# An adaptive-layernorm attention block on one core: five K accumulators for six, silu's steps on GpSimd, Q's weights as whole rows, the gate batch by batch

## The chip, the core and the metric

The kernel runs on one core of a Trainium2 chip. A core has five engines that run side by side, each with its own queue of instructions: TensorE (PE: matmuls, with weight loads shown as PEld), VectorE (DVE), ScalarE (ACT), GpSimd (POOL) and SyncE (SP), which here only issues DMAs. Matmuls write to PSUM, which this kernel uses as eight banks of 128 partitions x 512 fp32; all else lies in SBUF. The metric is the device time of one execution in microseconds.

## The reference

`x` is 2 x 256 x 1152 (B, N, D), `c` is 2 x 1152, all in bf16. The weights are `wqkv` (1152 x 3456), `wo` (1152 x 1152) and `w_mod` (1152 x 6912).

```python
mod = (silu(c) @ w_mod).reshape(B, 6, 1, D)
shift_a, scale_a, gate_a, shift_m, scale_m, gate_m = [mod[:, i] for i in range(6)]
h = layernorm(x, axis=-1) * (1 + scale_a) + shift_a
qkv = h @ wqkv
q, k, v = qkv[..., :D], qkv[..., D:2*D], qkv[..., 2*D:]
p = softmax(einsum('bqd,bkd->bqk', q, k) * D ** (-0.5), axis=-1)
a = einsum('bqk,bkd->bqd', p, v) @ wo
return x + gate_a * a
```

Three of the six rows of `mod` are used: shift, scale and gate of the attention.

## The kernel before

The 512 tokens (two batches of 256) are four tiles of 128; the 1152 features are nine blocks of 128, counted by k on the input side and by f on the output side.

*Front.* Each tile of x is centred (`centre`, line 227, on VectorE, with the mean from `bn` on VectorE or from `act_mean` on ScalarE), turned on TensorE in two halves (`transposes`, 233) and copied to `xcT` (`xcT_copy`, 240). silu(c) is computed by `silu_c` (191): one exponential on ScalarE, then three short VectorE steps, then a ScalarE copy that repeats it into `scT_rep`, the small operand of the modulation matmuls. The scale rows are matmuls of `wS` with it, in three parts of the features, PA (k 0 and 1), PB (2 to 4) and PC (5 to 8): `scale_open`, `scale_rows`, `scale_out`. `scaled` (273) multiplies `xcT` by a block's scale into `hTs`. The factor 1/std is not in it; it is applied later.

*K.* K's output is computed from `hTs` with k outermost, into six PSUM accumulators (`accs`, f 0 to 5). The other three blocks of f are computed for k 0 and 1 at once and parked in SBUF in the tile `held` (`pair_part` for f 6 and 7, `k_block` for f 8), and finished by `held_block` (425) for k 2 to 8. `k_part` runs a slice of tokens for k 0 and 1, `k_step` (292) all 512 tokens of one k.

*h.* 1/std of the four tiles is cut into three bf16 parts on VectorE, turned (`pT3`), masked and spread over the partitions by a matmul (`bc_ps`), and copied to `rstd_bc`, the last row of `held`. Then nine `normalised` steps write `hT`; the shift rows come from 36 matmuls with `wH` into `psH`, a VectorE transpose gives `shT`, and 18 `shifted` steps (VectorE and ScalarE) add them.

*Q, scores, V, output.* Q is nine blocks of nine matmuls (`q_block`, 456), each block to its end before the next. Q's weights and V's lie in six column chunks of 384 (`chunks_w`), loaded by `load_chunk`. Then the scores of both batches, the softmax (`scores`, `exps`, `probs`), whose first product also reads `rstd_bc`, and a DMA transpose (`turn`). Meanwhile TensorE runs twelve V groups, the attention products (`attnT`) and the output projection with `wO`.

*The gate.* `gate_steps` (480) accumulates silu(c) times `wG` on VectorE, nine steps for each batch of 128 x 1152; a GpSimd all-reduce over the partitions then sums it into `gate_bc`. The last 192 columns of the output use `wo_last`, `wO` times the gate, computed on GpSimd.

The order of every engine's instructions is that of the program: each engine's calls are recorded (line 76, which is why all instructions have that line) and pinned by `pin`. PSUM is one pool of six banks and two of one bank each. SyncE issues all large loads in one queue, in this order: x, wS and wK mixed, wH, Q's first chunk, then wG's three parts alternating with Q's other chunks, V's chunks, wO. The tiles `wG` and `wO` take the buffers of `wS` and `wH`, and `gate_bc` that of `held`.

What ties the all-reduces to the gate, on line 555 and following:

```python
    gate_done = dve_seq[-1].ins.name
    gate_bc = act.tile([P, B, D], F32, tag="gb")
    for b in range(B):
        ar = gps.partition_all_reduce(gate_bc[:, b, :], gacc[:, b, :], P, bass.bass_isa.ReduceOp.add)
        tc.add_manual_dep(ar.ins, gate_done, SYNC_SCHED, reason="keep gpsimd off the shared port")
```

Of the kernel before, what the change touches and what calls it, by code (L numbers as in the profile page):

```python
# [16 lines left out]
def kernel(  # L17
# [18 lines left out]
    FB = CW // P  # L36
# [3 lines left out]
    NACC = 6  # L40
    NPAIR = 2
    LASTF = KT - 1
# [58 lines left out]
    def one(t):  # L101
# [32 lines left out]
    chunk_cols = [vc * CW for vc in range(NCH)] + [2 * D + vc * CW for vc in range(NCH)]  # L134
    chunks_w = [wpool.tile([P, KT, CW], BF16, tag=f"wchunk{i}", name="wqv") for i in range(2 * NCH)]
# [15 lines left out]
    def load_chunk(i, k0, k1):  # L151
        c0 = chunk_cols[i]
        spq.dma_start(out=chunks_w[i][:, k0:k1, :], in_=wqkv_v[:, k0:k1, c0 : c0 + CW])
# [20 lines left out]
    load_chunk(0, 0, 5)  # L174
    load_chunk(0, 5, KT)

    junk_ps = psum_b.tile([P, 512], F32, tag="pb", name="junk_ps")
# [6 lines left out]
    e_sb = small.tile([P, B, KT], F32, tag="e_sb")  # L184
    scT_f = const.tile([P, KT, B], F32)
# [47 lines left out]
    def transposes(t, h, pool, tag):  # L233
        k0, k1 = HALF[h]
        tp = pool.tile([P, 5, P], BF16, tag=tag, name="tp")
# [16 lines left out]
    held = act.tile([P, NPAIR + 2, T], F32, tag="gb")  # L252
    rstd_bc = held[:, NPAIR + 1, :]

    psS = {}

    def scale_open(part, pool, tag):
        n = part[1] - part[0]
        ps = pool.tile([P, n, NR], F32, tag=tag, name="psS")
# [4 lines left out]
    def scale_rows(part, kk0, kk1):  # L264
        for kk in range(kk0, kk1):
            for j in range(*part):
                ten.matmul(psS[part][:, j - part[0], :], lhsT=wS[:, kk, j * P : (j + 1) * P], rhs=sc_rhs(kk),
                           start=False, stop=(kk == KT - 1), skip_group_check=True)
# [18 lines left out]
    def pair_part(ps, k, sl):  # L287
        for i in range(NPAIR):
            ten.matmul(ps[:, i, :], lhsT=wk(k, NACC + i), rhs=hTs[:, k, sl],
                       start=(k == 0 and i == 0), stop=(k == KA - 1), skip_group_check=True)  # L290

    def k_step(k):
        for f in range(NACC):
            ten.matmul(accs[f], lhsT=wk(k, f), rhs=hTs[:, k, :],
                       start=False, stop=(k == KT - 1), skip_group_check=True)
# [11 lines left out]
    fillers(11)  # L307
    silu_c()
    mv0 = bn(0)
# [4 lines left out]
    scale_open(PA, psum_a, "pa")  # L314
    transposes(0, 0, psum, "mm")
    transposes(0, 1, psum, "mm")
    fillers(2)
    scale_rows(PA, 0, 4)
    transposes(1, 0, psum, "mm")
    transposes(1, 1, psum, "mm")  # L320
    xcT_copy(0, 0, True)
    xcT_copy(1, 0, True)
    centre(2, nmean[:, 2:3], ALU.add)
    xcT_copy(0, 1, False)
    fillers(2)
    scale_rows(PA, 4, KT)
    xcT_copy(1, 1, False)
    scaled(0, tok(0), psS[PA][:, 0, 0:1])
    scale_out(PA)
    scaled_b(1, 0)  # L330


    accs = [psum.tile([P, T], F32, tag="mm", name="acc") for _ in range(NACC)]
    k_part(0, tok(0))
    transposes(2, 0, psum_b, "pb")
    xcT_copy(2, 0, False)
# [3 lines left out]
    for k in range(KA):  # L340
        scaled(k, one(2), s1p[:, k, 1:2])
# [3 lines left out]
    centre(3, mv3[:, 0:1], ALU.subtract)  # L345
    ps_b0 = psum_a.tile([P, NPAIR, N], F32, tag="pa", name="psE")
    pair_part(ps_b0, 0, tok(0))
    k_part(1, tok(0))
    pair_part(ps_b0, 1, tok(0))
    transposes(2, 1, psum_b, "pb")  # L350
    sca.copy(out=held[:, 0:NPAIR, tok(0)], in_=ps_b0)
    xcT_copy(2, 1, False)
    act_var(1)
    for k in range(KA):
        k_part(k, one(2))


    scale_open(PB, psum_a, "pa")
    scale_rows(PB, 0, 4)
    transposes(3, 0, psum_b, "pb")  # L360
    xcT_copy(3, 0, True)
    scale_rows(PB, 4, KT)
    for k in range(KA):
        scaled(k, one(3), s1p[:, k, 1:2])
    scale_out(PB)
    transposes(3, 1, psum_b, "pb")
    xcT_copy(3, 1, False)
    act_var(2)
    gps.tensor_copy(out=var[:, 0:1], in_=mv0[:, 1:2])
    gps.tensor_copy(out=var[:, 3:4], in_=mv3[:, 1:2])  # L370
    gps.tensor_scalar_add(out=rstd, in0=var, scalar1=EPS)
    gps.tensor_tensor(out=rstd, in0=rstd, in1=neg_half, op=ALU.pow)
    for k in range(KA):
        k_part(k, one(3))
    for k in range(*PB):
        for b in range(B):
            scaled_b(k, b)
    ps_b1 = psum_b.tile([P, NPAIR, N], F32, tag="pb", name="psE")
    for k in range(KA):
        pair_part(ps_b1, k, tok(1))  # L380
    f8 = psum_a.tile([P, T], F32, tag="pa", name="psL")
    k_block(LASTF, f8, 0, KA)
    sca.copy(out=held[:, 0:NPAIR, tok(1)], in_=ps_b1)
    sca.copy(out=held[:, NPAIR, :], in_=f8)


# [3 lines left out]

    parts = const.tile([P, TT, 3], BF16)
    rest = const.tile([P, TT], F32)
    vec.tensor_copy(out=parts[:, :, 0], in_=rstd)
    vec.tensor_tensor(out=rest, in0=rstd, in1=parts[:, :, 0], op=ALU.subtract)
    vec.tensor_copy(out=parts[:, :, 1], in_=rest)
    vec.tensor_tensor(out=rest, in0=rest, in1=parts[:, :, 1], op=ALU.subtract)
    vec.tensor_copy(out=parts[:, :, 2], in_=rest)
    scale_open(PC, psum_b, "pb")
    scale_rows(PC, 0, KT)
    pT3 = psum_a.tile([NP3, P], BF16, tag="pa", name="pT3")  # L400
    ten.transpose(pT3, parts.rearrange("p t i -> p (t i)"), ident)
    masked = const.tile([NP3, TT, P], BF16)
    scale_out(PC)
    for b in range(B):
        scaled_b(PC[0], b)
    vec.tensor_tensor(out=masked, in0=pT3.unsqueeze(1).to_broadcast([NP3, TT, P]), in1=mask, op=ALU.mult)
    for k in range(PC[0] + 1, PC[1]):
        for b in range(B):
            scaled_b(k, b)
    k_step(PC[0] - 1)  # L410
    k_step(PC[0])
    bc_ps = psum_a.tile([P, T], F32, tag="pa", name="bc_ps")
# [8 lines left out]
    for k in range(PC[0] + 1, KT):  # L421
        k_step(k)
    for f in range(NACC):
        evac(False, qkT[:, KT + f, :], accs[f])
    def held_block(i, f, pool, tag):
        ps = pool.tile([P, T], F32, tag=tag, name="psK")
        k_block(f, ps, KA, KT)
        vec.tensor_tensor(out=qkT[:, KT + f, :], in0=ps, in1=held[:, i, :], op=ALU.add)

    held_block(0, NACC, psum_a, "pa")  # L430


    psH = psum_b.tile([P, KT, 32], F32, tag="pb", name="psH")
# [19 lines left out]
    held_block(1, NACC + 1, psum, "mm")  # L453
    held_block(2, LASTF, psum, "mm")

    def q_block(f):
        wt, off = chunks_w[f // FB], f % FB * P
        ps = psum.tile([P, T], F32, tag="mm", name="psQ")
        for k in range(KT):
            ten.matmul(ps, lhsT=wt[:, k, off : off + P], rhs=hT[:, k, :], start=(k == 0), stop=(k == KT - 1))  # L460
        return ps
# [16 lines left out]
    gates = [(b, kt) for g in range(0, KT, 3) for b in range(B) for kt in range(g, g + 3)]  # L478
# [11 lines left out]
    for f in range(KT):  # L490
        evac(False, qkT[:, f, :], q_block(f))
# [3 lines left out]
    for b in range(B):  # L495
        s_ps = psum.tile([P, NQ, N], F32, tag="mm")
# [39 lines left out]
    def v_group(gidx):  # L536
        t, vc = divmod(gidx, NCH)
        wt = chunks_w[NCH + vc]
        ps = psum.tile([P, CW], F32, tag="mm")
# [4 lines left out]
    gate_steps(13)  # L544
# [12 lines left out]
    for b in range(B):  # L557
        ar = gps.partition_all_reduce(gate_bc[:, b, :], gacc[:, b, :], P, bass.bass_isa.ReduceOp.add)
# [93 lines left out]
```

## Time and profile before

| what | value |
|---|---|
| time, median of 3 runs | 98.85 us (98.83 to 100.47) |
| the profiled execution: its own time | 98.85 us |
| its span from first to last instruction | 97.1 us |
| granted TensorE clock in it | 1.0 |
| first K matmul | 9.99 us |
| K's step k=2 begins | 16.45 us |
| shift rows (`psH`) begin | 28.96 us |
| Q begins, ends | 33.21, 50.9 us |
| V groups begin; attention; output projection | 54.6; 72.2; 76.1 us |
| last matmul ends | 93.9 us |

Times in the profile count from the start of the span. A row of a timeline has the start, the time in us, the engine, the line, the operation, output and inputs, the shapes, how many were merged, and in brackets how long the engine was idle before and what ended that. TensorE's matmuls overlap: a row's time is that of the first start to the last end, so starts are what to compare. "SPq" rows are DMA issues; the time to landing is counted from the start of the issue.

### The profile page before, as it was taken

The page shows a single profiled execution, that of the slowest core. Times are in us where ns is not written, and L with a number is a line of the kernel's source. Part 1 is how long each engine was busy: PE and PEld are TensorE (multiplying, and loading weights), DVE is VectorE, ACT ScalarE, POOL GpSimd, SP SyncE. Part 2 cuts the span into 40 slices and gives each one's busy share as a digit, 9 for nine tenths or more (in the row PEclk, how much of TensorE's full clock was granted, in tenths as well). Part 3 has the DMA queues.
Part 4 walks back from the last instruction along what each step waited for, and adds up shares of the span by engine and source line. Part 5 has one row for each costly group of instructions (what it writes and reads, how often), then busy time and mean ns, then how long its engine had stood idle before and what let it go on. Part 6 is the DMA issues. An engine that isn't in the chain of part 4 may idle for free.

```text
span 97.1 us, 1688 instructions
## 1 busy us (share of the span) xinstructions
PE 90.9 (94%) x666; PEld 53.6 (55%) x670; DVE 70.2 (72%) x136; ACT 32.5 (33%) x66; POOL 24.3 (25%) x28
## 2 busy tenths in 40 slices
PE   3979899999999999999999999999999999999960
PEld 1327886463445444444458766656668766666660
DVE  1296876273999999999995899960229587779880
ACT  5098298302094722242221472331115400000000
POOL 6500001600000000000000000029999940059700
PEclk9999999999999999999999999999999999999999
DMA  2999999999999999999999962200000000311212
GB/s 29 336 306 368 352 368 354 387 392 393 392 345 364 350 359 354 356 357 326 330 343 387 390 224 58 54 7 0 0 0 0 0 0 0 128 49 72 108 56 79
DMA packets 18311, 21.31 MB, mean 219 GB/s; under 512 B 2176, under 2 KB 12800, under 8 KB 18304
## 3 DMA queue, kind: packets, MB, share of 16 engines
q1 hardware_dynamic: 17888, 21.19, 65.0%
q8 instruction: 5, 0.08, 0.3%
q10 hardware_dynamic: 416, 0.02, 0.3%
q14 instruction: 2, 0.02, 0.1%
HBM read 19.76 MB, written 1.18 MB: 216 GB/s over the span
## 4 chain that ended last, share of the span: by engine, by line
PE 86%; DVE 5%; DMA 3%; ACT 1%; issue 1%; DVEq 0%
PE ps L76 39%; PE psQ L76 18%; PE acc L76 12%; PE psK L76 5%; PE s_ps L76 4%; DMA c_sb<-in_c_dram 3%; PE tp L76 2%; PE psS L76 2%; DVE stats L76 1%; PE psH L76 1%; PE psE L76 1%; DVE o_sb L76 1%; PE junk_ps L76 1%; DVE ga L76 1%; ACT xcT L76 1%
## 5 line engine op out<-in xcount | busy, mean ns | idle before, releaser
L76 POOL PARTITION_ALL_REDUCE gate_bc<-gacc x2 | 13.7, 6887 | 46.2 <-DVE gacc L76 46.2
L76 DVE SCALAR_TENSOR_TENSOR gacc<-wG,scT_f,gacc 128x1152 f32<-128x1152 bf16 x16 | 22.3, 1417 | 0.4
L76 PE MATMUL ps<-wqv,hT 128*128 128x384 bf16 x108 | 17.7, 326 | 0.0
L76 PE MATMUL psQ<-hT,wqv 128*128 128x512 bf16 x80 | 17.6, 379 | 0.1
L76 PE MATMUL ps<-wO,attnT 128*128 128x384 bf16 (+1 forms) x108 | 17.0, 320 | 0.0
L76 PEld LDWEIGHTS <-attnT 128*128 128x128 bf16 x126 | 11.3, 98 | 6.4
L76 PEld LDWEIGHTS <-hT 128*128 128x128 bf16 x108 | 10.6, 98 | 6.9
L76 PEld LDWEIGHTS <-wK 128*128 128x128 bf16 x109 | 9.4, 98 | 8.1 <-issue 1.1
L76 PE MATMUL acc<-hTs,wK 128*128 128x512 bf16 (+2 forms) x77 | 12.6, 313 | 0.6 <-DVE hTs L76 0.4
L76 PEld LDWEIGHTS <-wqv 128*128 128x128 bf16 x81 | 7.9, 98 | 9.6
L76 ACT CAST qkT<-psQ 128x512 bf16<-128x512 f32 x9 | 5.3, 585 | 12.9 <-PE psQ L76 12.9
L76 DVE TENSOR_TENSOR ga<-ps,gate_bc 128x384 f32<-128x384 f32 (+1 forms) x12 | 6.5, 540 | 3.5 <-PE ps L76 3.5
L76 ACT CAST v_sb<-ps 128x384 bf16<-128x384 f32 x10 | 4.7, 475 | 10.7 <-PE ps L76 10.7
L76 DVE TENSOR_TENSOR o_sb<-ga,x_sb 128x384 bf16<-128x384 f32 (+1 forms) x12 | 7.2, 601 | 0.4
L76 PE MATMUL junk_ps<-junk 128*128 128x512 bf16 x15 | 6.1, 562 | 1.5 <-DVE junk L76 1.5
L76 POOL TENSOR_TENSOR wo_last<-wO,gate_bc 128x192 bf16<-128x192 bf16 x9 | 5.6, 659 | 7.3 <-issue 7.3
L76 DVE TENSOR_TENSOR hT<-hTs,held 128x512 bf16<-128x512 bf16 x9 | 5.5, 688 | 1.6 <-ACT held L76 1.6
L76 ACT CAST o_sb<-ps 128x64 bf16<-128x64 f32 x1 | 0.2, 212 | 17.3 <-PE ps L76 17.3
L76 PEld LDWEIGHTS <-junk 128*128 128x128 bf16 (+2 forms) x19 | 2.1, 121 | 5.8 <-issue 4.2
L76 DVE CAST v_sb<-ps 128x384 bf16<-128x384 f32 x2 | 1.1, 558 | 5.6 <-PE ps L76 5.6
L76 PE MATMUL psK<-hTs,wK 128*128 128x512 bf16 x20 | 4.8, 380 | 0.1
L76 DVE CAST attnT<-ps 128x512 bf16<-128x512 f32 (+1 forms) x6 | 3.5, 603 | 1.7 <-PE ps L76 1.7
(77 smaller groups left out, 87.5 us busy)
## 6 DMA issues: line engine op xcount, KB each, us to landing
wqv<-in_wqkv_dram SPq DMA_DIRECT2D x5, 864.0 KB, 11.3
wH<-in_w_mod_dram SPq DMA_DIRECT2D x3, 864.0 KB, 13.3
wG<-in_w_mod_dram SPq DMA_DIRECT2D x3, 864.0 KB, 12.1
wO<-in_wo_dram SPq DMA_DIRECT2D x3, 864.0 KB, 9.7
wK<-in_wqkv_dram SPq DMA_DIRECT2D x5, 288.0 KB, 6.9
x_sb<-in_x_dram SPq DMA_DIRECT2D x4, 288.0 KB, 3.8
wK<-in_wqkv_dram SPq DMA_DIRECT2D x2, 576.0 KB, 10.4
out_dram<-o_sb SPq DMA_DIRECT2D x3, 288.0 KB, 2.1
```

The lines of the kernel that those rows point to most:

```text
L76: r = fn(*a, **k)
```

## The change

- *PSUM:* five banks in the pool, and three single ones (BA, BB, BC); `bank` hands them out. After the held blocks, Q, scores, V, attention and projection take the eight in a ring.
- *K:* five accumulators; four blocks of f are parked after k 0 and 1, in pairs for each batch, and finished by four held blocks, two before the shift rows and two after.
- *Front:* one filler more at the start and four fewer later. silu's addition, product and copy go from VectorE and ScalarE to GpSimd; the mask is made after them. Tile 2 is turned behind the scale rows of PA. Tile 3's mean comes from a ScalarE sum of 640 columns and a VectorE sum of 512. Tile 2's variance goes from ScalarE to VectorE. PB's and PC's scale rows run in one piece, and 1/std is cut into its parts on GpSimd.
- *Q:* its weights are one tile loaded in three groups of whole rows ahead of wG, and the first four blocks run with k outermost.
- *Gate:* all nine steps of batch 0 come first, and its all-reduce is issued ahead of batch 1's last eight steps; the extra dependency is gone.

```diff
-    NACC = 6
-    NPAIR = 2
-    LASTF = KT - 1
+    NACC = 5
+    NPARK = KT - NACC
...
-    psum = ctx.enter_context(tc.tile_pool(name="psum", bufs=6, space=PSUM))
+    psum = ctx.enter_context(tc.tile_pool(name="psum", bufs=5, space=PSUM))
...
+    psum_c = ctx.enter_context(tc.tile_pool(name="psum_c", bufs=1, space=PSUM))
+    MM, BA, BB, BC = (psum, "mm"), (psum_a, "pa"), (psum_b, "pb"), (psum_c, "pc")
+    ring = [MM] * 5 + [BA, BB, BC]
+    turn_no = [0]
+
+    def bank(shape, name, dtype=None, where=None):
+        if where is None:
+            where = ring[turn_no[0] % len(ring)]
+            turn_no[0] += 1
+        return where[0].tile(shape, dtype or F32, tag=where[1], name=name)
...
+    def load_q(k0, k1):
+        spq.dma_start(out=wQ[:, k0:k1, :], in_=wqkv_v[:, k0:k1, 0:D])
+
+    def load_v(i):
+        c0 = 2 * D + i * CW
+        spq.dma_start(out=chunks_w[i], in_=wqkv_v[:, :, c0 : c0 + CW])
...
-    load_chunk(0, 0, 5)
-    load_chunk(0, 5, KT)
+    for k0, k1 in ((0, 2), (2, 5), (5, KT)):
+        load_q(k0, k1)
...
         sca.activation(out=e_sb, in_=c_sb, func=ACT.Exp, scale=-1.0)
-        vec.tensor_scalar_add(out=e_sb, in0=e_sb, scalar1=1.0)
-        vec.reciprocal(out=e_sb, in_=e_sb)
-        vec.tensor_tensor(out=scT_f.rearrange("p k b -> p b k"), in0=c_sb, in1=e_sb, op=ALU.mult)
-        sca.copy(out=scT_rep, in_=scT_f.unsqueeze(2).to_broadcast([P, KT, NR // B, B]))
+        gps.tensor_scalar_add(out=e_sb, in0=e_sb, scalar1=1.0)
+        vec.reciprocal(out=r_sb, in_=e_sb)
+        gps.tensor_tensor(out=scT_f.rearrange("p k b -> p b k"), in0=c_sb, in1=r_sb, op=ALU.mult)
+        gps.tensor_copy(out=scT_rep, in_=scT_f.unsqueeze(2).to_broadcast([P, KT, NR // B, B]))
...
+    scale_open(PC, BB)
+    scale_rows(PC, 0, KT)
+    scale_out(PC)
+    for k in range(*PC):
         for b in range(B):
             scaled_b(k, b)
...
+    k_step(PC[0] - 1)
+    k_step(PC[0])
+    k_step(PC[0] + 1, 0, 3)
+    pT3 = bank([NP3, P], "pT3", BF16, BA)
...
+    held_block(0, BA)
+    held_block(1, BC)
...
-    load_mod(wG, 2, 0, 3, 0, D)
-    load_chunk(1, 0, KT)
-    load_mod(wG, 2, 3, 6, 0, D)
-    load_chunk(2, 0, KT)
-    load_mod(wG, 2, 6, KT, 0, D)
-    load_chunk(3, 0, KT)
-    load_chunk(4, 0, KT)
-    load_chunk(5, 0, KT)
+    for k0 in range(0, KT, 3):
+        load_mod(wG, 2, k0, k0 + 3, 0, D)
+    for i in range(NCH):
+        load_v(i)
...
-    gates = [(b, kt) for g in range(0, KT, 3) for b in range(B) for kt in range(g, g + 3)]
+    gates = [(b, kt) for b in range(B) for kt in range(KT)]
...
+    QACC = 4
+    q_acc = [bank([P, T], "psQ", where=MM) for _ in range(QACC)]
+    for k in range(KT):
+        for f in range(QACC):
+            ten.matmul(q_acc[f], lhsT=wq(k, f), rhs=hT[:, k, :], start=(k == 0), stop=(k == KT - 1))
...
-    gate_steps(13)
+    gate_bc = act.tile([P, B, D], F32, tag="gb")
+
+    def spread(b):
+        gps.partition_all_reduce(gate_bc[:, b, :], gacc[:, b, :], P, bass.bass_isa.ReduceOp.add)
+
+    gate_steps(9)
     scores(0)
     exps(0)
     scores(1)
...
     gate_steps(1)
     probs(1)
     turn(1)
+    spread(0)
     gate_steps(len(gates))
-    gate_done = dve_seq[-1].ins.name
-    gate_bc = act.tile([P, B, D], F32, tag="gb")
-    for b in range(B):
-        ar = gps.partition_all_reduce(gate_bc[:, b, :], gacc[:, b, :], P, bass.bass_isa.ReduceOp.add)
-        tc.add_manual_dep(ar.ins, gate_done, SYNC_SCHED, reason="keep gpsimd off the shared port")
+    spread(1)
```

More of the change, by code (lines that the diff above doesn't have):

```diff
@@ L231, with transposes @@
     tps = {}
-    def transposes(t, h, pool, tag):
+    def transposes(t, h, where):
         k0, k1 = HALF[h]
-        tp = pool.tile([P, 5, P], BF16, tag=tag, name="tp")
+        tp = bank([P, 5, P], "tp", BF16, where)
         for k in range(k0, k1):
@@ L251, with scale_open @@
     qkT = act.tile([P, 2 * KT, T], BF16)
-    held = act.tile([P, NPAIR + 2, T], F32, tag="gb")
-    rstd_bc = held[:, NPAIR + 1, :]
+    held = act.tile([P, NPARK + 1, T], F32, tag="gb")
+    rstd_bc = held[:, NPARK, :]
     psS = {}
-    def scale_open(part, pool, tag):
+    def scale_open(part, where):
         n = part[1] - part[0]
-        ps = pool.tile([P, n, NR], F32, tag=tag, name="psS")
+        ps = bank([P, n, NR], "psS", where=where)
         ten.matmul(ps.rearrange("p j r -> p (j r)"), lhsT=junk[0:1, :P], rhs=ones_row[0:1, 0 : n * NR],
@@ L262, in scale_open, with scale_rows @@
         psS[part] = ps
[L264 to L268, printed above, removed]
+    def scale_rows(part, kk0, kk1, js=None):
+        for j0, j1 in [part] if js is None else js:
+            for kk in range(kk0, kk1):
+                for j in range(j0, j1):
+                    ten.matmul(psS[part][:, j - part[0], :], lhsT=wS[:, kk, j * P : (j + 1) * P], rhs=sc_rhs(kk),
+                               start=False, stop=(kk == KT - 1), skip_group_check=True)
     def scale_out(part):
@@ L285, in k_part, with pair, pair_part, park @@
                        start=(k == 0 and sl.start == 0), stop=False, skip_group_check=True)
-    def pair_part(ps, k, sl):
-        for i in range(NPAIR):
-            ten.matmul(ps[:, i, :], lhsT=wk(k, NACC + i), rhs=hTs[:, k, sl],
-                       start=(k == 0 and i == 0), stop=(k == KA - 1), skip_group_check=True)
-    def k_step(k):
-        for f in range(NACC):
+    def pair(i, b, where):
+        return bank([P, 2, N], "psE", where=where), NACC + 2 * i, tok(b)
+    def pair_part(pr, k):
+        ps, f0, sl = pr
+        for i in range(2):
+            ten.matmul(ps[:, i, :], lhsT=wk(k, f0 + i), rhs=hTs[:, k, sl],
+                       start=(k == 0 and i == 0), stop=(k == KA - 1), skip_group_check=True)
+    def park(pr):
+        ps, f0, sl = pr
+        sca.copy(out=held[:, f0 - NACC : f0 - NACC + 2, sl], in_=ps)
+    def k_step(k, f0=0, f1=NACC):
+        for f in range(f0, f1):
             ten.matmul(accs[f], lhsT=wk(k, f), rhs=hTs[:, k, :],
@@ L313 @@
     act_mean(2)
[L314 to L317, printed above, removed]
+    scale_open(PA, BA)
+    transposes(0, 0, MM)
+    transposes(0, 1, MM)
+    xcT_copy(0, 0, True)
+    xcT_copy(0, 1, False)
+    transposes(1, 0, MM)
+    transposes(1, 1, MM)
     scale_rows(PA, 0, 4)
-    transposes(1, 0, psum, "mm")
-    transposes(1, 1, psum, "mm")
-    xcT_copy(0, 0, True)
+    centre(2, nmean[:, 2:3], ALU.add)
     xcT_copy(1, 0, True)
[L323 to L326, printed above, removed]
     xcT_copy(1, 1, False)
+    scale_rows(PA, 4, KT, js=[(0, 1), (1, 2)])
     scaled(0, tok(0), psS[PA][:, 0, 0:1])
+    transposes(2, 0, BB)
+    transposes(2, 1, BC)
     scale_out(PA)
-    scaled_b(1, 0)
-    accs = [psum.tile([P, T], F32, tag="mm", name="acc") for _ in range(NACC)]
-    k_part(0, tok(0))
-    transposes(2, 0, psum_b, "pb")
-    xcT_copy(2, 0, False)
+    xcT_copy(2, 0, True)
+    xcT_copy(2, 1, False)
+    scaled(0, one(2), s1p[:, 0, 1:2])
+    scaled(1, tok(0), s1p[:, 1, 0:1])
+    scaled(1, one(2), s1p[:, 1, 1:2])
+    accs = [bank([P, T], "acc", where=MM) for _ in range(NACC)]
+    k_part(0, tok(0))
+    k_part(0, one(2))
+    pr10 = pair(0, 0, BC)
+    pair_part(pr10, 0)
+    H3 = 5 * P
+    sca.activation(out=xc[:, 3, 0:H3], in_=x_sb[:, 3, 0:H3], func=ACT.Copy, accum_out=ssum[3])
+    half3 = small.tile([P, 1], F32, tag="half3", name="half3")
+    vec.reduce_sum(out=half3, in_=x_sb[:, 3, H3:D], axis=AX.X)
+    vec.tensor_scalar(out=nmean[:, 3:4], in0=half3, scalar1=ssum[3], scalar2=-1.0 / D, op0=ALU.add, op1=ALU.mult)
+    centre(3, nmean[:, 3:4], ALU.add)
+    k_part(1, tok(0))
+    pair_part(pr10, 1)
+    k_part(1, one(2))
+    pr20 = pair(1, 0, BA)
+    park(pr10)
+    transposes(3, 0, BB)
+    pair_part(pr20, 0)
+    pair_part(pr20, 1)
+    transposes(3, 1, BC)
+    xcT_copy(3, 0, True)
+    park(pr20)
+    xcT_copy(3, 1, False)
+    for k in range(KA):
+        scaled(k, one(3), s1p[:, k, 1:2])
     st3 = small.tile([P, NCH, 6], F32, tag="stats", name="stats")
@@ L340 @@
     for k in range(KA):
-        scaled(k, one(2), s1p[:, k, 1:2])
+        k_part(k, one(3))
+    scale_open(PB, BA)
+    scale_rows(PB, 0, KT)
+    scale_out(PB)
+    for k in range(*PB):
+        for b in range(B):
+            scaled_b(k, b)
     bn_part(3, st3, 2)
@@ L344 @@
     vec.bn_aggr(out=mv3, in_=st3)
[L345 to L352, printed above, removed]
-    act_var(1)
[L354 to L368, printed above, removed]
+    mv2 = bn(2)
+    pr11, pr21 = pair(0, 1, BB), pair(1, 1, BC)
+    for pr in (pr11, pr21):
+        for k in range(KA):
+            pair_part(pr, k)
+        park(pr)
+    act_var(1)
     gps.tensor_copy(out=var[:, 0:1], in_=mv0[:, 1:2])
     gps.tensor_copy(out=var[:, 3:4], in_=mv3[:, 1:2])
+    gps.tensor_copy(out=var[:, 2:3], in_=mv2[:, 1:2])
@@ L381 @@
[L381 to L384, printed above, removed]
-    for k in range(PB[0], PB[1] - 1):
-        k_step(k)
     parts = const.tile([P, TT, 3], BF16)
     rest = const.tile([P, TT], F32)
-    vec.tensor_copy(out=parts[:, :, 0], in_=rstd)
-    vec.tensor_tensor(out=rest, in0=rstd, in1=parts[:, :, 0], op=ALU.subtract)
-    vec.tensor_copy(out=parts[:, :, 1], in_=rest)
@@ L396 @@
[L396 to L400, printed above, removed]
+    gps.tensor_copy(out=parts[:, :, 0], in_=rstd)
+    gps.tensor_tensor(out=rest, in0=rstd, in1=parts[:, :, 0], op=ALU.subtract)
+    gps.tensor_copy(out=parts[:, :, 1], in_=rest)
+    gps.tensor_tensor(out=rest, in0=rest, in1=parts[:, :, 1], op=ALU.subtract)
@@ L410 @@
-    k_step(PC[0] - 1)
-    k_step(PC[0])
-    bc_ps = psum_a.tile([P, T], F32, tag="pa", name="bc_ps")
+    k_step(PC[0] + 1, 3)
+    k_step(PC[0] + 2, 0, 2)
+    bc_ps = bank([P, T], "bc_ps", where=BC)
     ten.matmul(bc_ps, lhsT=junk[:NP3, :P], rhs=masked.rearrange("p t n -> p (t n)"), start=True, stop=True)
@@ L420 @@
         normalised(k)
-    for k in range(PC[0] + 1, KT):
+    k_step(PC[0] + 2, 2)
+    for k in range(PC[0] + 3, KT):
         k_step(k)
@@ L424, with held_block @@
         evac(False, qkT[:, KT + f, :], accs[f])
[L425 to L433, printed above, removed]
+    def held_block(i, where):
+        ps = bank([P, T], "psK", where=where)
+        k_block(NACC + i, ps, KA, KT)
+        vec.tensor_tensor(out=qkT[:, KT + NACC + i, :], in0=ps, in1=held[:, i, :], op=ALU.add)
+    held_block(0, BA)
+    held_block(1, BC)
+    psH = bank([P, KT, 32], "psH", where=BB)
     wH_v = wH.rearrange("p kk (k j c) -> p kk k j c", k=KT, j=4)
@@ L452, with wq @@
         shifted(i)
[L453 to L461, printed above, removed]
+    held_block(2, MM)
+    held_block(3, BB)
+    def wq(k, f):
+        return wQ[:, k, f * P : (f + 1) * P]
     wG = wmpool.tile([P, KT, D], BF16, tag="wS")
     wO = wmpool.tile([P, KT, D], BF16, tag="wH")
-    load_mod(wG, 2, 0, 3, 0, D)
-    load_chunk(1, 0, KT)
-    load_mod(wG, 2, 3, 6, 0, D)
-    load_chunk(2, 0, KT)
-    load_mod(wG, 2, 6, KT, 0, D)
-    load_chunk(3, 0, KT)
-    load_chunk(4, 0, KT)
-    load_chunk(5, 0, KT)
+    for k0 in range(0, KT, 3):
+        load_mod(wG, 2, k0, k0 + 3, 0, D)
+    for i in range(NCH):
+        load_v(i)
     for k0 in range(0, KT, 3):
@@ L488, in gate_steps @@
                                          in1=gacc[:, b, :], op0=ALU.mult, op1=ALU.add)
-    for f in range(KT):
-        evac(False, qkT[:, f, :], q_block(f))
+    turn_no[0] = 4
+    QACC = 4
[3 more added lines that the diff above has]
+            ten.matmul(q_acc[f], lhsT=wq(k, f), rhs=hT[:, k, :], start=(k == 0), stop=(k == KT - 1))
+    for f in range(QACC):
+        evac(False, qkT[:, f, :], q_acc[f])
+    for f in range(QACC, KT):
+        ps = bank([P, T], "psQ")
+        for k in range(KT):
+            ten.matmul(ps, lhsT=wq(k, f), rhs=hT[:, k, :], start=(k == 0), stop=(k == KT - 1))
+        evac(False, qkT[:, f, :], ps)
     s_tiles = []
     for b in range(B):
-        s_ps = psum.tile([P, NQ, N], F32, tag="mm")
+        s_ps = bank([P, NQ, N], "s_ps")
         for i in range(NQ):
```

56 lines of the change are left out of this document (23 added, 33 removed).

## The prediction, made before the changed kernel ran

> **What bounds the kernel now.** I read the page first (busy shares, the 40 slices), then the chain that ended last, then the DMA issues with their landings, then the timelines of the engines where the diff works.
>
> ```profile
> span 97.1 us, 1688 instructions
> PE 90.9 (94%) x666; PEld 53.6 (55%) x670; DVE 70.2 (72%) x136; ACT 32.5 (33%) x66; POOL 24.3 (25%) x28
> ...
> PE   3979899999999999999999999999999999999960
> ...
> DMA  2999999999999999999999962200000000311212
> ...
> PE 86%; DVE 5%; DMA 3%; ACT 1%; issue 1%; DVEq 0%
> ```
>
> PE is nearly full from slice 4 on and is 86% of the chain; DMA is full to slice 23 (56 us). So up to some point PE may be fed by DMA at its limit. The timeline of PE around the shift rows, and the landing of wH's third part, show where:
>
> ```profile
> 28.96 1.29 PE L76 MATMUL psH<-wH,scT_rep 128*32 128x288 bf16 x36
> 30.18 3.19 PE L76 MATMUL psK<-hTs,wK 128*128 128x512 bf16 x13
> 33.21 0.59 PE L76 MATMUL psQ<-hT,wqv 128*128 128x512 bf16 x2
> ...
> 15.12 2.28 SPq L76 DMA_DIRECT2D wH<-in_w_mod_dram  x1
> ...
> DMA to landing us min/median/max: 14.5/14.5/14.5
> ```
>
> Issued at 15.12, landed 14.5 later: 29.6. The last third of the 36 psH matmuls starts at 28.96 + 2/3 of 1.22 = 29.75. PE reaches wH's last rows 0.1 us after they land. From 33.21 (Q) to 93.9 PE has no gap: 80 psQ in 17.65 us, 108 V matmuls in 17.71, 108 of the output projection in 16.99, each 512 columns 0.216. Nothing in the diff takes columns from that stretch.
>
> **The change part by part.** The sum is made against the profiled run: 98.85 us, span 97.1, 1.75 around it; 98.85 is also the median.
>
> *First 15 us.* Four fillers (two pairs of 0.43) leave the path, scT_rep's 0.43 leaves ScalarE, so the means of tiles 1 and 2 come 0.4 to 0.6 earlier. Along VectorE: bn and centre(0) end about 7.05 as before, centre(1) 7.5, first copy 7.95, centre(2) 8.4, copy 8.75, scaled(0) 8.8 to 9.1; first K matmul 9.15 (before 9.99). Tile 2's nine transposes (0.5) lie before it, behind the scale rows, under scaled(0). The same 9,216 columns of k 0 and 1 follow: five accumulators and four parked blocks instead of six, two and one. With tile 3's mean at 11.1 (640 columns on ScalarE, 0.7 + 0.2; a 512-column reduce by the row of mx 0.69, 0.3 to 0.7), step k=2 begins at 15.0; before 16.45. Parking costs ScalarE four copies of 0.58 for three, under matmuls.
>
> GpSimd's silu: add and multiply by its 128x4 row 0.24 each, the 288-column copy between ScalarE's 0.43 and 1.0 (1.5 times the 0.66 of 192 columns); scT_rep is ready by 5.5 to 6.2 and PE asks at 8.1. The mask's memset and selects (0.51 + 1.33) move from 2.0 to 5.8–7.7, beside centre(0) and (1): 0 to 0.6 each. I take 0; 1.2 is covered by the next wait.
>
> *What PE's 1.4 us buys: nothing.* The second part of scale's rows PC is issued at 8.64 and lands 10.4 later, 19.05. PE now gets there at 17.7 and waits 1.35. From there after and before differ: 19.1 + 20 rows 0.5 + wK(4), landing 9.98 + 9.8 = 19.8 → five matmuls 1.08 → 20.95; wK(5:7) lands 11.40 + 9.9 = 21.3 → 21.4. Then 20 K matmuls and 14 of held blocks at 0.216 (7.34), turn 0.17, bc_ps 0.41: psH at 29.3 against 28.96, because five accumulators leave 34 matmuls behind that landing where six leave fewer (two blocks of seven now stand before psH, and only ten, not twelve, matmuls of k 2 and 3 before the wait). psH 1.22 and 14 psK 3.03: Q at 33.6. Loss 0.4 (bounds 0 to 0.8: the landings could move; below 0 by 0.1 at most, as wH lands at 29.6).
>
> VectorE's chain beside it: bc_ps 24.2, ScalarE's copy to 25.25, nine normalised 5.42, two adds 1.2, shT 0.5, first shifts: hT[0] ready 33.0, 0.6 before Q; later k need 0.3 each where PE takes 0.86, since Q now runs k outermost over four accumulators. rstd's three parts on GpSimd (five steps of some 0.28) end at 21.4 to 22, wanted at 23.1. Nothing.
>
> *Q's weights.* 864 KB in 768-byte rows took 2.7 us (wG's first part lands 34.6, the chunk behind it 26.40 + 10.9 = 37.3), in whole rows 2.3 (wH, wG). wQ's parts land at 31.2, 33.5 and 36.5; Q wants them at 33.6, 35.3 and 37.9. wG now stands behind all of wQ: 38.8, 41.1, 43.4 instead of 34.6 for the first. wV lands 46 to 51.5, wanted at 55.
>
> *The gate.* Nine steps of batch 0: 38.8 + 0.85 + 8 × 1.40 = 50.9, before the scores (53.3): covered. Then scores, exps, probs, one step of 0.82 (for 1.42), and eight SCALAR_TENSOR_TENSOR at 1.40 after probs(1) (59.1): 70.4, where before four ended at 64.8. Behind them on VectorE stand two v_sb casts and attnT's. The first cast's tile is used again, in a ring of eight banks, by the fifth attention block at 74.3; so up to 74.2 − 0.56 there is 3.3 us of cover.
>
> *The all-reduce of batch 0* loses its wait for all gates. gate_bc shares its buffer with held, which the second scores product reads, so it starts not at 50.9 but at 56.0, and lasts 6.85: to 62.9, beside VectorE's work. No all-reduce of before stands beside such work:
>
> ```profile
> 65.00 13.69 POOL L76 PARTITION_ALL_REDUCE gate_bc<-gacc  x2 [46.21 <-DVE gacc L76]
> ...
> 86.61 1.88 POOL L76 TENSOR_TENSOR wo_last<-wO,gate_bc 128x192 bf16<-128x192 bf16 x3
> ...
> 87.20 0.87 DVE L76 TENSOR_TENSOR o_sb<-ga,x_sb 128x384 bf16<-128x384 f32 x1
> ...
> 78.42 0.56 DVE L76 TENSOR_TENSOR o_sb<-ga,x_sb 128x384 bf16<-128x384 f32 x1
> ```
>
> The nearest row with both engines at work is wo_last: o_sb takes 0.87 beside it and 0.56 alone, and the GpSimd instruction in progress next grows too (1.88 for three, where the quickest are 0.55 each): they take turns by whole instructions. Upper bound: VectorE stands still for the 6.85. Lower bound 0 (a gain is excluded: nothing gets shorter): the o_sb at 78.42 overlaps the last 0.27 of the second all-reduce and keeps its 0.56, though spans on GpSimd are rough. I take the upper bound; wo_last is the row with both overlapping fully.
>
> Its price: nmx(1), pn(0), the 0.82 step and pn(1) move from 56.7 to 62.9, the eight steps end at 76.6, the first cast at 77.2. PE, wanting that bank at 74.3, stands 2.9. The second all-reduce then ends at 83.5; wo_last follows 7.33 later as now, 90.8 to 96.5, against a last projection chunk at 96.2: covered but for some 0.3 of o_sb steps that share those turns at the tail. V's evictions wait for exps(1) until 64; the ring has room to 66.8.
>
> Sum: 97.1 + 0.4 + 2.9 + 0.3 = 100.7, and 1.75 around it: 102.4.
>
> The Trainium skill, "SBUF — State Buffer", section "Who interferes with whom", says that VectorE's fast one-input modes and its two-input forms share one pair of ports with GpSimd, and that whoever starts first holds it for the whole instruction. By that rule the time is this 102.4; the row of 87.20 agrees, the one of 78.42 does not bear it out.
>
> **The rivals.**
> 1. *Not slower: the all-reduce holds nothing, or takes turns in short pieces.* For it: 78.42. Then the gate ends by 70.4 to 73.5, inside the cover: 97.1 + 0.4 + 1.75 = 99.2. It decides at 73.6 for the end of the eight steps.
> 2. *Only two-input forms stand still.* The trace shows only such a one (o_sb) slowed; ga beside wo_last keeps 0.56. Then probs run, the eight steps wait from 59.1 to 62.9 and end 74.1, cast 74.7: PE loses 0.4 to 0.5, 99.7.
> 3. *PE's clock falls in the new 1.35 us wait.* The slices show full speed throughout, the longest gap before being 0.58 at 6.5. If it halved for some 3 us of full work, K's end moves 1.5 to 2: 101. Against it: short waits of 0.4 to 0.6 cost nothing.
> 4. *Landings come earlier by 1 us.* Then wH frees PE and up to 0.6 is gained: 98.3. Against: rate is 350 to 390 GB/s in every slice, and no issue before wH changes.
>
> **How the numbers follow.** Whole hold 0.47; rival 1 0.24; rival 2 0.18; clock or an early delay past the 1.35 cover 0.06 (mostly over 2%); earlier landings 0.05, of which over 2% 0.03 with whatever I do not see. Slower by over 2% (above 100.8; 2% is about what a measurement of this kernel can tell from no change): 0.47 + 0.05 = 0.52. Within: 0.44. Faster: 0.04. The likeliest case gives 102.4, its own range 101.4 to 103.2 (K's 0 to 0.8, the hold 6.2 to 6.9, the tail). The range must reach to rivals 1 and 2: from 98.9 to 103.2.
>
> **What would show it.** In the changed kernel: first K matmul near 9.2 and k=2 near 15; PE idle some 1.3 us before psS's last 20 rows at 19.1; psH at 29.3; Q at 33.6; wG's first landing near 38.8; the first all-reduce starting right after the second p_f product, and nmx or pn before a gap of some 6 us on VectorE; a PE gap near 74 to 77 that waits for a v_sb cast. Wrong at once if VectorE shows no gap between 56 and 63, or if PE passes 74 without one; and if Q starts before 33, the landings were not the bound.

## The result, and the profile after

The changed kernel takes 102.96 us (median of 4 runs, 102.03 to 103.61) against 98.84 for the kernel before (4 runs on the same chip). Each kernel's slowest run, 103.61 and 100.47, counts as slow, and ratios here and below are of fast runs alone: 1.0389, 95% interval 1.029 to 1.0488. The profiled execution took 103.51, span 101.5. First its page: PE's busy share and granted clock in 40 slices of 2.54 us.

```profile
PE   4989999889999999999999999999937999999970
...
PEclk9999999999999999999999999999997599999999
```

Before, PE's row had nothing but nines here. It now has a hole in slices 30 and 31 (the 3 and the 7), and the clock row shows 7 and 5 in slices 31 and 32, just behind the hole.

The timeline of PE through K, with waits in brackets:

```profile
18.63 0.67 PE L84 MATMUL psS<-scT_rep,wS 128*128 128x32 bf16 x20 [0.18 <-DMA wS<-in_w_mod_dram]
...
20.89 1.90 PE L84 MATMUL acc<-hTs,wK 128*128 128x512 bf16 x8 [0.47 <-DMA wK<-in_wqkv_dram]
...
29.02 1.29 PE L84 MATMUL psH<-wH,scT_rep 128*32 128x288 bf16 x36
...
33.54 4.70 PE L84 MATMUL psQ<-hT,wQ 128*128 128x512 bf16 x21
```

k=2 begins 0.97 earlier than before (15.48 for 16.45), and Q still starts 0.33 later (33.54 for 33.21). The lead is spent in waits for landings by the time `psH` begins (29.02 for 28.96). Most of the rest, 0.28, is lost behind `psH`: the fourth held block gets `psH`'s bank BB, which VectorE's transpose reads until 31.98, and its first matmul starts at 32.03, 0.49 after the one ahead of it, where 0.216 is the rule; in the kernel before that pair has 0.216. The gap is too short for the view to mark it.

Next VectorE from the second scores product, and GpSimd; the first row is the kernel before:

```profile
56.27 0.17 DVE L76 TENSOR_SCALAR nmx<-mx 128x2 f32<-128x2 f32 x1
```
```profile
55.15 0.69 DVE L84 TENSOR_TENSOR p_f<-s_ps,held 128x512 f32<-128x512 f32 x1 [0.35 <-PE s_ps L84]
...
56.60 4.60 DVE L84 TENSOR_SCALAR nmx<-mx 128x2 f32<-128x2 f32 x1
...
61.30 1.90 DVE L84 TENSOR_SCALAR pn<-p_f,rinv 128x256 bf16<-128x256 f32 x2
...
64.57 11.59 DVE L84 SCALAR_TENSOR_TENSOR gacc<-wG,scT_f,gacc 128x1152 f32<-128x1152 bf16 x8
76.08 1.01 DVE L84 CAST v_sb<-ps 128x384 bf16<-128x384 f32 x2
```
```profile
56.07 6.99 POOL L84 PARTITION_ALL_REDUCE gate_bc<-gacc  x1 [34.22 <-ACT p_f L84]
76.26 6.83 POOL L84 PARTITION_ALL_REDUCE gate_bc<-gacc  x1 [13.20 <-DVE gacc L84]
90.56 5.57 POOL L84 TENSOR_TENSOR wo_last<-wO,gate_bc 128x192 bf16<-128x192 bf16 x9 [7.47 <-issue]
```

The all-reduce of batch 0 starts at 56.07, just behind the product that is the last to read `held`; it ends at 55.84. (The bracket names a ScalarE step on `p_f` because that ended a little later, at 55.93; the run with a buffer of its own, below, shows that `held` is what counts.) Behind the product and the maximum, which keep their 0.69, comes a VectorE step that writes two numbers per partition: it takes 4.60 us, where it took 0.17 before. It ends at 61.12 to 61.2, 5.05 to 5.1 after the all-reduce's start; a reciprocal and the first `pn` run, and the second `pn` (1.90 for two, 0.62 before) is held to about 63.06, the all-reduce's end. The eight gate steps end at 76.16, and the cast behind them is what PE waits for. The first row is again the kernel before:

```profile
72.17 4.09 PE L76 MATMUL ps<-pT,v_sb 128*128 128x256 bf16 x36
```
```profile
72.50 1.91 PE L84 MATMUL ps<-pT,v_sb 128*128 128x256 bf16 x16
76.68 3.52 PE L84 MATMUL ps<-pT,v_sb 128*128 128x256 bf16 x20 [2.27 <-DVE v_sb L84]
79.99 17.53 PE L84 MATMUL ps<-wO,attnT 128*128 128x384 bf16 x108
```

After the wait the 20 attention matmuls take 3.52, where 36 took 4.09 before, and the projection's 108 take 17.53 for 16.99. The busy times of the stretch from 77.70 to 81.10 say why (length, then PE, weight loads, VectorE, ScalarE, GpSimd, granted clock, DMA share, GB/s):

```profile
77.70:81.10 3.40, 3.40 (x17) 2.21 (x15) 2.54 (x5) 1.17 (x2) 3.40 (x1) 0.50 0.00 0
```

For 3.4 us from 77.7 the clock is half. Work that needs 1.7 at full speed takes 3.4: 1.7 lost. From 81.1 on it is full again. The account: 0.33 at Q + 2.27 waited + 1.7 at half clock = 4.3; the span grew by 4.4.

The theory to test: **H**, the all-reduce, put beside `nmx(1)` and `pn` by `gate_bc` sharing `held`'s buffer, holds VectorE, and the eight gate steps with the cast behind them hand that on to PE. Its rivals: **B**, the batch order does it without any hold (eight steps instead of four stand behind the softmax); and parts elsewhere in this large change.

### The profile page after: what moved, and what is told of

Read it like the earlier page. It is cut to its first block, busy times and chain, and to the rows that moved or that the text cites. A ratio compares the mean times of both kernels' runs of the same rounds, so it can differ in the third digit from the quotient of the medians.

```text
span 101.5 us, 1694 instructions
## 1 busy us (share of the span) xinstructions
PE 92.7 (91%) x663; PEld 54.2 (53%) x667; DVE 78.2 (77%) x137; ACT 30.7 (30%) x64; POOL 26.6 (26%) x36
## 4 chain that ended last, share of the span: by engine, by line
PE 46%; DVE 30%; DMA 15%; SPq 5%; issue 1%; ACT 1%; DVEq 0%
PE ps L84 20%; PE psQ L84 17%; DMA wK<-in_wqkv_dram 15%; DVE gacc L84 12%; DVE hT L84 5%; SPq L84 5%; DVE nmx L84 5%; PE s_ps L84 4%; PE acc L84 3%; DVE pn L84 2%; PE psK L84 2%; DVE qkT L84 1%; DVE o_sb L84 1%; DVE ga L84 1%; DVE p_f L84 1%
## 5 line engine op out<-in xcount | busy, mean ns | idle before, releaser
L84 PE MATMUL ps<-wV,hT 128*128 128x384 bf16 x108 | 17.7, 326 | 0.0
L84 PE MATMUL psQ<-hT,wQ 128*128 128x512 bf16 x80 | 17.6, 379 | 0.1
L84 PE MATMUL ps<-wO,attnT 128*128 128x384 bf16 (+1 forms) x108 | 17.5, 326 | 0.0
L84 PEld LDWEIGHTS <-wQ 128*128 128x128 bf16 x81 | 7.9, 98 | 9.5
L84 PE MATMUL acc<-hTs,wK 128*128 128x512 bf16 (+2 forms) x63 | 11.1, 312 | 0.7 <-DMA wK<-in_wqkv_dram 0.5
L84 PE MATMUL ps<-pT,v_sb 128*128 128x256 bf16 x36 | 5.4, 318 | 2.3 <-DVE v_sb L84 2.3
L84 PE MATMUL psK<-hTs,wK 128*128 128x512 bf16 x27 | 6.5, 379 | 0.2
L84 PE MATMUL junk_ps<-junk 128*128 128x512 bf16 x12 | 5.0, 599 | 1.5 <-DVE junk L84 1.5
L84 PEld LDWEIGHTS <-v_sb 128*128 128x128 bf16 x36 | 4.0, 112 | 3.4 <-issue 2.4
```

Source lines behind the costliest of these rows:

```text
L84: r = fn(*a, **k)
```

## The experiments

Each diff is against the changed kernel unless said, and shortened ("..."); every ratio is to the kernel before.

**Gate's part alone** (the kernel before, with the batch order and the free all-reduce and nothing else of the change):

```diff
-    gates = [(b, kt) for g in range(0, KT, 3) for b in range(B) for kt in range(g, g + 3)]
+    gates = [(b, kt) for b in range(B) for kt in range(KT)]
...
-    gate_steps(13)
...
+    gate_steps(9)
...
+    spread(0)
     gate_steps(len(gates))
...
+    spread(1)
```

> The kernel before with the gate's part of the change alone: gate by batch, first all-reduce ahead of batch 1's last eight steps, no extra wait. H: the all-reduce starts after the second p_f product near 55.7, VectorE stands some 5.8 us in nmx and pn, the eight steps end near 75.8, PE waits 2 us or more for a v_sb cast (its ring of six wants that bank near 73.1), and 101.5 to 103.5 us. F: near 98.9.

Measured: 103.85, median of 101.93, 103.79, 103.91 and 105.55; these scatter too far for an interval. VectorE and PE in the profiled execution (103.91):

```profile
56.36 4.60 DVE L76 TENSOR_SCALAR nmx<-mx 128x2 f32<-128x2 f32 x1
```
```profile
76.44 4.88 PE L76 MATMUL ps<-pT,v_sb 128*128 128x256 bf16 x28 [3.15 <-DVE v_sb L76]
```

The 4.60, the late cast (75.84) and the gap come with this part alone. Its one run at mean clock 1.0 took 101.93, the three at 0.977 to 0.979 took 103.79 or more; the median lies above the 101.5 to 103.5 expected.

**A buffer of its own** for the gate's row (K's weights, done by then), so that batch 0's all-reduce can start when its gate is ready:

```diff
-    wK = wpool.tile([P, KT, D], BF16)
+    wK = wpool.tile([P, KT, D], BF16, tag="wK")
...
-    gate_bc = act.tile([P, B, D], F32, tag="gb")
+    gate_bc = wpool.tile([P, B, D], F32, tag="wK")
```

> The changed kernel with gate_bc in K's weight buffer, free by then, instead of held's: the first all-reduce needs only batch 0's nine steps. H: it starts near 51.2 and holds VectorE's one-input steps to about 56.2 and again to about 58.1; nmx(0), due at 54.6, ends near 56.2, nmx(1) near 58; only 1.4 us is lost, the eight steps end near 71.8, inside the cover, no PE gap, 99.2 to 99.4 us. B: no change, near 102.5. If a hold hits all VectorE steps whatever they read, p_f(0), due at 53.2, waits too, and some 3 us is lost: eight steps end at 73.5, about 99.4.

Measured: 99.26 (98.91 to 100.17, 10 runs), ratio 1.004 [1.0008, 1.0072]. GpSimd, then VectorE:

```profile
50.80 6.85 POOL L84 PARTITION_ALL_REDUCE gate_bc<-gacc  x1 [28.79 <-DVE gacc L84]
```
```profile
53.04 0.69 DVE L84 TENSOR_TENSOR p_f<-s_ps,held 128x512 f32<-128x512 f32 x1 [2.45 <-PE s_ps L84]
...
54.49 1.45 DVE L84 TENSOR_SCALAR nmx<-mx 128x2 f32<-128x2 f32 x1
...
57.28 0.40 DVE L84 TENSOR_SCALAR nmx<-mx 128x2 f32<-128x2 f32 x1
...
71.23 1.01 DVE L84 CAST v_sb<-ps 128x384 bf16<-128x384 f32 x2
```

The all-reduce is as long as ever, but starts 5.3 us earlier, 0.21 behind the last of batch 0's gate steps. Its first 2.2 us lie beside VectorE's wait for the scores. It holds `nmx(0)` until 55.85, again 5.05 after its start (5.04 to 5.05 in all six runs in which `nmx` meets the first part of an all-reduce), and `nmx(1)` a little until its end; it doesn't hold the product at 53.04, which reads PSUM, nor the maximum behind it (0.69 as ever). The cast comes at 71.23 instead of 76.08, PE has no gap, the clock is 1.0 and the 4 us are gone. The batch order is still there, so B falls as the main cause. Left over is 0.4%.

**Both all-reduces behind the last gate step**, the batch order kept:

```diff
-        gps.partition_all_reduce(gate_bc[:, b, :], gacc[:, b, :], P, bass.bass_isa.ReduceOp.add)
+        return gps.partition_all_reduce(gate_bc[:, b, :], gacc[:, b, :], P, bass.bass_isa.ReduceOp.add)
...
-    spread(0)
     gate_steps(len(gates))
-    spread(1)
+    gate_done = dve_seq[-1].ins.name
+    for b in range(B):
+        tc.add_manual_dep(spread(b).ins, gate_done, SYNC_SCHED, reason="after all gates")
```

> The changed kernel with both all-reduces again waiting for the last gate step; everything else of the change stays, the batch order of the gate too. If the hold is the cause (theory H: a GpSimd all-reduce in progress keeps VectorE's steps from running): nmx(1) takes 0.17 us, the eight steps end near 70.4, PE has no gap between 72 and 77, granted clock 1.0, and 99.2 us, that is 0.3 to 0.4 over the kernel before, which is K's part. If the batch order of the gate is the cause (rival B: eight steps instead of four stand behind the probabilities): still a PE gap near 74 and over 101. If the front and K are the cause (rival F): over 101 with Q later than 34.

Measured: 102.59 (102.17 to 102.86), ratio 1.0376 [1.0346, 1.0406]. A miss: the gap at 74 goes, as H said, but not the time, and the granted clock of the profiled run is 0.978 instead of 1.0. GpSimd, VectorE and PE's end; the rows of line 76 are the kernel before:

```profile
86.02 5.64 POOL L76 TENSOR_TENSOR wo_last<-wO,gate_bc 128x192 bf16<-128x192 bf16 x9 [7.33 <-issue]
```
```profile
71.06 13.69 POOL L84 PARTITION_ALL_REDUCE gate_bc<-gacc  x2 [48.80 <-DVE gacc L84]
91.65 5.54 POOL L84 TENSOR_TENSOR wo_last<-wO,gate_bc 128x192 bf16<-128x192 bf16 x9 [6.90 <-issue]
```
```profile
79.14 4.30 DVE L84 TENSOR_TENSOR o_sb<-ga,x_sb 128x384 bf16<-128x384 f32 x1
...
83.94 0.56 DVE L84 TENSOR_TENSOR o_sb<-ga,x_sb 128x384 bf16<-128x384 f32 x1
```
```profile
92.93 0.67 PE L76 MATMUL ps<-wo_last,attnT 128*128 128x128 bf16 x9
```
```profile
93.65 0.33 PE L84 MATMUL ps<-wo_last,attnT 128*128 128x128 bf16 x3
94.23 0.22 PE L84 MATMUL ps<-wo_last,attnT 128*128 128x128 bf16 x1 [0.26 <-POOL wo_last L84]
```

There is a second chain: the gate's end, both all-reduces, some 7 us in which GpSimd does nothing the profile shows, `wo_last`, the last chunk. Before, it ran from 64.8 to 91.7 and PE came at 92.93. From 70.8 and with 13.69 of all-reduces it ends at 97.2, and PE waits for it step by step. From 93.0 to 96.4 PE is busy for 1.80 of 3.40 us, its longest wait 0.60, and from 96.4 on the clock is half. In the changed kernel this chain ends at 96.1, beside a PE that is late itself (97.36), so no wait shows it there.

**All casts of V and attention on ScalarE**, the hold left in:

```diff
-        evac(gidx >= 7 and gidx % 2 == 0, v_sb[:, t, vc * CW : (vc + 1) * CW], ps)
+        evac(False, v_sb[:, t, vc * CW : (vc + 1) * CW], ps)
...
-            evac(gi % 2 == 0, attnT[:, dv0 : dv0 + ndv, b * N : (b + 1) * N], ps[:, :ndv, :])
+            evac(False, attnT[:, dv0 : dv0 + ndv, b * N : (b + 1) * N], ps[:, :ndv, :])
```

> The changed kernel with every cast of v_sb and of attnT on ScalarE; batch 0's all-reduce keeps its place and holds VectorE as before, so the eight gate steps still end near 76. If the whole price came through the v_sb cast that stands behind them, TensorE has no gap at 74 to 77 and the time is 99.2 to 99.6. My theory from the run in which both all-reduces waited for the gate: there is a second chain, gate's end -> second all-reduce (76.3 to 83.1) -> some 7 us of idle GpSimd -> wo_last (90.5 to 96.1). No gap at 74 to 77 then, but TensorE comes to the last chunk's weights about 2 us earlier than wo_last does and waits there: 101 to 101.8. No half clock around 78 in either case.

Measured: 101.79 (101.43 to 102.37), ratio 1.0281 [1.0252, 1.0311]; batch 1's all-reduce runs from 77.21 to 84.04. GpSimd and PE:

```profile
91.22 5.72 POOL L84 TENSOR_TENSOR wo_last<-wO,gate_bc 128x192 bf16<-128x192 bf16 x9 [7.17 <-issue]
```
```profile
94.22 0.49 PE L84 MATMUL ps<-wo_last,attnT 128*128 128x128 bf16 x5
95.32 0.22 PE L84 MATMUL ps<-wo_last,attnT 128*128 128x128 bf16 x1 [0.61 <-POOL wo_last L84]
```

The gap and the half clock behind it are gone, and PE waits at the end instead: from the last chunk's first matmul to its end it takes 3.3 us, where 1.0 was enough before. So taking the cast away is worth about 1 us of the 4, as the second chain foretold; the hold reaches the end by two ways, one right behind the other.

**PE busy through the wait**: 20 products into the bank that PE is about to write, which the next ones overwrite.

```diff
+            if b == 0 and gi == 3:
+                for _ in range(20):
+                    ten.matmul(ps[:, 0, :], lhsT=v_sb[:, 0, dv0 * P : (dv0 + 1) * P], rhs=pT_sbs[0][:, 0, :],
+                               start=True, stop=True)
```

> The changed kernel with 20 products of 256 columns more, written to the fourth attention block's bank and overwritten by it, so that TensorE has work (2.2 us) while it waits for the cast. The hold and the lateness of the cast stay (eight steps end near 76.2). If the half clock after the wait is a price of its own (theory C: 1.7 us of the 4.4): granted clock 1.0, attention and projection at 0.109 and 0.163 a matmul at once, 101.3 to 102.0 us. If the clock falls whatever TensorE does then: no change, 102.0 to 103.6.

Measured: 102.57 (102.3 to 102.67), ratio 1.0368 [1.0349, 1.0388]. PE:

```profile
77.47 2.34 PE L84 MATMUL ps<-pT,v_sb 128*128 128x256 bf16 x20 [0.20 <-DVE v_sb L84]
79.65 16.99 PE L84 MATMUL ps<-wO,attnT 128*128 128x384 bf16 x108
```

Full speed behind the wait: 2.34 and 16.99 for 3.52 and 17.53. That much says that PE's standing still costs the clock. The time did not come down to 101.3 to 102.0: in the profiled run Q starts at 34.21, 0.67 later than in the changed kernel's, and PC's second part, issued 0.83 later there, landed at 19.27 instead of 18.59. From Q's start to the last matmul's end it takes 63.2 us, the changed kernel 64.8: nearly all of the 1.7 is gone there, and the late Q hides part of it in the total. It fits that the changed kernel's runs at mean clock 0.997 took 102.03 and 102.4, those at 0.983 took 103.51 and 103.61.

**Without the loads of scale's last columns**, in both kernels: the rows of PC are computed from the columns of PA and PB, so K is computed from another scale there, with as many matmuls. First the run with a buffer of its own for the gate:

```diff
-    load_s(PC, 0, 4)
-    load_s(PC, 4, KT)
...
-                    ten.matmul(psS[part][:, j - part[0], :], lhsT=wS[:, kk, j * P : (j + 1) * P], rhs=sc_rhs(kk),
+                    ten.matmul(psS[part][:, j - part[0], :], lhsT=wS[:, kk, j % 5 * P : (j % 5 + 1) * P], rhs=sc_rhs(kk),
```

> The run whose gate row has a buffer of its own (99.26, no hold) without the loads of scale's last columns (wS part PC); their product rows read the columns of parts PA and PB instead, so the rows computed there are other ones and the number of matmuls stays. If the landings bound K's stage in the changed order (the prediction's 'what the 1.4 us buys: nothing'), all later landings come about 1 us earlier, Q starts at 32.3 to 32.7 instead of 33.4 and the time is 98.2 to 98.6. If K's stage is bound by TensorE, Q stays at 33.3 and the time at 99.2.

Measured: 98.2 (98.11 to 98.46), ratio 0.9938 [0.9917, 0.9958]. The same in the kernel before:

> The kernel before with the same loads left out and the same rows computed from other columns. There TensorE comes to these rows after they have landed, and only wH's last part is landing-bound, by 0.1 us or so. So 98.6 to 98.9, Q at 33.0 to 33.2. If the kernel before is landing-bound as well, it gains as much as the changed one: 98.0 to 98.3.

Measured: 98.75 (98.48 to 100.31), ratio 0.9981 [0.9966, 0.9995]. PE in the two, changed order first:

```profile
32.97 3.40 PE L84 MATMUL psQ<-hT,wQ 128*128 128x512 bf16 x15
```
```profile
32.96 3.40 PE L76 MATMUL psQ<-hT,wqv 128*128 128x512 bf16 x15
```

The kernel before barely moves; the changed order gains 1.06 us by the medians, 0.57 by the profiled runs, 0.43 by Q's start (expected 0.7 or more; without the waits it is PE's own work that holds Q at 32.97, and the 0.28 for bank BB, which this run has too). So K is bound by the landings in the changed order and not in the old one, the sign and not quite the size as expected.

**Work into the wait**: two parked blocks do their k 2 and 3 in the wait for PC's second part, in banks BA and BC; `pT3` and `bc_ps` move to BB, the third held block goes ahead of the shift rows, and the fourth takes BA instead of BB. Against the run with a buffer of its own:

```diff
-    scale_rows(PC, 0, KT)
+    scale_rows(PC, 0, 4)
+    early = [bank([P, T], "psK", where=w) for w in (BA, BC)]
+    for i in range(2):
+        for k in (KA, KA + 1):
+            ten.matmul(early[i], lhsT=wk(k, NACC + i), rhs=hTs[:, k, :], start=(k == KA), stop=False,
+                       skip_group_check=True)
+    scale_rows(PC, 4, KT)
...
```

> The run whose gate row has a buffer of its own, with four K matmuls more (two parked blocks' k 2 and 3) put in the wait ahead of the second part of scale's last columns, where TensorE has nothing to do. They leave the stretch behind that landing: 4 matmuls of 0.216, 0.86 us. By the landing theory Q starts at 32.6 to 32.9 (wH's last part lands near 29.0 and may take some of it back) and the time is 98.4 to 98.8, at or just below the kernel before. If TensorE's own work or the fill of the banks bounds that stretch, it stays at 99.2.

Measured: 98.33 (98.08 to 98.41, 6 runs), ratio 0.9941 [0.9922, 0.996]: 0.6% below the kernel before, small, but the interval leaves out 1. PE:

```profile
17.86 0.57 PE L84 MATMUL psS<-scT_rep,wS 128*128 128x32 bf16 x16
18.27 1.02 PE L84 MATMUL psK<-hTs,wK 128*128 128x512 bf16 x4
19.13 0.66 PE L84 MATMUL psS<-scT_rep,wS 128*128 128x32 bf16 x20
...
32.46 3.83 PE L84 MATMUL psQ<-hT,wQ 128*128 128x512 bf16 x17
```

No wait is marked between 17.86 and Q, which starts 0.75 earlier than in the kernel before and a little earlier than expected. The gain lies ahead of `psH`: from k=2 to `psH`, without the seven matmuls moved there, it takes 12.5 us, as in the kernel before, and 13.2 in the run with a buffer of its own. With these two edits the change is worth 0.5 us: a wait at a landing hid its gain, and the hold buried it.

## Why the prediction was right

*The likeliest case came true*, 102.4 forecast, 102.96 measured, and by its mechanism: gate's part alone makes the loss, a buffer of its own takes it away.

*K buys nothing: right, but the 0.33 that Q lost for the 0.4 forecast is in part luck.* The lead of 1.4 us at k=2 (0.97 in the end) was to be lost at PC's second part. It landed at 18.59 instead of 19.05, so the wait there was 0.18 and the next, for wK's last blocks, 0.47. With that `psH` began at 29.02, 0.28 ahead of the forecast 29.3. The prediction had nothing for the wait behind it, for bank BB, and that took 0.28 as well. The two runs without PC's loads confirm that the stretch up to `psH` waits for landings in the new order only.

*The mask's selects beside the centring, taken as 0: wrong, and without effect.* The two centring steps took 0.65 and 0.88 instead of some 0.51; the cover that the prediction named held, with 0.18 us of waiting left over.

*The whole hold, bounds 0 and 6.85, upper end taken: right in its result, not in its form.* The all-reduce did not hold all of VectorE to its end (62.9 forecast, 63.06 measured). It held in two pieces: 5.05 us, a release in which two short steps ran, then the rest. In the first piece stood the one-input `nmx`, and `o_sb`, which reads two operands from SBUF (4.30 with both all-reduces behind the gate, 3.03 with ScalarE's casts); in the second piece one-input `pn` or `nmx` stood, while `o_sb` at 83.94 kept its 0.56 with the all-reduce running to 84.75. That settles the row at 78.42 that the prediction set against its own choice: it lay in the second piece. The Trainium skill ("SBUF — State Buffer", section "Who interferes with whom") has VectorE's fast one-input modes contend with any GpSimd instruction and its two-input forms only with one that reads SBUF. The rows agree, if the all-reduce reads SBUF in the first piece and only writes in the second; no run shows directly what it does in them. The Trainium skill's lock for a whole instruction isn't what they show: VectorE got in between. It is a close race there: in the run with PE busy through the wait the first `pn`, 5.23 after the all-reduce's start as in the changed kernel, was held itself (1.76 for 0.35), and the all-reduce took 6.85 instead of 6.99.

*Its price: mis-sized by parts that cancelled.* The eight steps ended at 76.16 instead of 76.6, so PE stood 2.27 instead of 2.9. On the other side the prediction had no term for the half clock behind this wait, 1.7 us. Rival 3 had priced such a halving at 1.5 to 2, but tied it to a wait of 1.35 at 17.7, which came out at 0.18. In this kernel the waits of 0.2 to 0.6 left the clock at full, as its counter-argument said, and the one of 2.27 did not; but the row of short waits at the end of the run with both all-reduces behind the gate was followed by half clock. That the median came within 0.6 of the forecast is partly luck. A mean clock of 0.983 is what 3.4 us at half clock make of a span of 101.5, and 0.997 leaves no room for them; the two runs at 0.997, 102.03 and 102.4, which have no trace, would be those that the prediction's terms describe.

*The tail: right for this kernel, by little.* The 0.3 for `o_sb` did not come: from the last matmul's end to the span's end it is 3.2 us in both. `wo_last` ended at 96.13 and PE took it at 97.36. Two runs show how near that was: with both all-reduces behind the gate, or with the casts on ScalarE, PE waited for `wo_last`.

*Rivals 1 and 2 fell* with `nmx` at 4.60, a one-input step standing for the first piece of the hold. Rival 4: landings came 0.46 earlier at PC, but wH's last part at 29.57 as before. (The prediction's rate of 350 to 390 GB/s "in every slice" reads that row too narrowly: slices 4 to 23 of the kernel before show 326 to 393.)

## What to carry to other kernels

When a step is freed of a wait on paper, look up what else its output buffer waits for: here the shared buffer, and not the removed dependency, chose the moment, and it chose the one place where VectorE was needed. Before undoing a loss at the place where the profile shows it, follow the late work to its other readers: with the cast taken away, or the hold moved off the softmax to behind the gate, the price came back at `wo_last`. And time won in front of a landing is worth nothing until work is moved from behind that landing to before it.

## What the hardware showed that was not expected

- A VectorE step of two numbers per partition can take 4.60 us beside a GpSimd all-reduce of 128 x 1152, where it takes 0.17 alone. A large duration on a small shape is the sign of a hold, and nothing in the waits names it: the waits of PE name only the cast far behind.
- A PE wait of 2.27 us was followed by 3.4 us at half clock, beginning 1 us after work resumed; behind the wait of 3.15, in the run of gate's part alone, the same 3.4 us began 0.6 after. The Trainium skill ("TensorE: Matmul & The Clock Gate", Part 1) speaks of idle gaps above some 3.4 us and of a free-running window of that length. The length at half clock agrees; the gap that sufficed here was shorter. That the place of a gap in such a window decides would fit the runs of one kernel at 0.983 and at 0.997; it was not tried. Nor need it be one gap: waits of at most 0.60, which left PE busy for 1.80 of 3.40 us, were followed by half clock too.
- After an all-reduce GpSimd is idle for 6.7 to 7.8 us before `wo_last`, in every run, before and after, with nothing to wait for that the profile shows. The kept traces list two MODIFY_POOL_CONFIG and a DRAIN on its queue right behind the last all-reduce (from 83.04 in the changed kernel, 78.64 in the kernel before), which no view counts as busy. What fills the time stays open.
